# Transposes of probabilities and gate factors as two half blocks of 64 query rows, on halves of TensorE's array

## The chip, the cores and the metric

The kernel runs on one core of a Trainium2 chip. The time is the device time of one execution in microseconds (us), the median of repeated runs. Engines are named as the profile names them: PE is TensorE (PEld its weight loads), DVE is VectorE, ACT is ScalarE, POOL is GpSimd, SP is SyncE, which issues the DMAs.

## The reference, cut to what matters

Three layers follow one another on 2 sequences of 768 tokens, all in float32. First comes attention with 8 heads of 64 channels, over a window of 15 keys to either side and over the maxima or means of 24 blocks of 32 keys. Then comes a mixture of 4 experts, each a causal attention of its own with 64 channels, of which each token takes the best two, weighted by gates. Last is a feed-forward layer with token shift, 512 to 1024 to 512, squared ReLU and a sigmoid gate.

```python
a = np.exp(scores_all - max); a = a / (a.sum(-1) + 1e-9)      # layer 1: windowed and block keys together
x = np.matmul(a, v_all)
...
a = softmax(causal(scale * q @ k.T)); ye = a @ v @ wo[e]      # layer 2, expert e
out += mask * w * ye
...
k = np.maximum(xk @ w_k, 0.0); v = k * k @ w_v                # layer 3
return 1 / (1 + np.exp(-(xr @ w_r))) * v
```

## The kernel before, in words

**Turning the probabilities.** Softmax is computed with the query rows on the partitions. The product with the values wants the keys there. So each block of probabilities is turned by TensorE: a matmul with the block as weights and an identity as the moving operand, whose result lies in PSUM and has to be copied to SBUF before it can be used.

**Stage one** (`stage1`, L1331) works through 12 tiles of 128 queries. For each, `stage1_scores` (L556) makes the scores of 8 heads, 4 heads in each of two groups called `par`, with 120 keys each. `stage1_softmax` (L600) makes probabilities of them. `stage1_trans` (L633) turns the 4 blocks of one `par` into one PSUM bank (L652), which one copy of 512 columns takes out. `stage1_out` (L657) multiplies with the values (L670).

**The experts' attention** (`attention`, L819) works through 4 chunks of 384 queries, and in each through 2 pairs of experts (`ep`). `scores` (L827) makes the scores of both experts of a pair, which lie on the two halves of the partitions, with matmuls on half the rows of the array each (L845). `weights` (L870) makes the gate factors, one value for each query and expert, spread over 128 columns, and turns three blocks of them (L886). `attend` (L894) takes the blocks of probabilities in groups of three, two groups in the first chunk of a sequence and five in the second. `tr` (L899) turns one group of one expert into one bank (L905), and one copy of 384 columns takes it out. `vmm` (L920) multiplies a few groups with the values (L931), the two experts on the two halves of the array's columns.

**After that** come the output projection (L973), the gate of the last layer (`rec`, L1125), its first product (`hid`, L1176) and its second (`duo`, L1263), with splitting of operands into a high and a low part on VectorE, ScalarE and GpSimd (L371 to L381 and others). No block is turned there.

**Shapes of the array.** Each TensorE step notes a mode: full (128 x 128), half (two halves of the columns), rows (two halves of the rows) or quarter. Products with weights and all turns are full, the scores of the experts are rows, the products with values half, the scores of stage one quarter.

**The order of the work** is not that of the program. `Plan.op` (L240) only notes steps, numbered as they are noted, with their buffers, and `Plan.run` (L270) issues them in the order of the list `ORDER` (L53). An entry divided by four is the number of the step; the remainder chooses among the engines that the step allows. A step is issued as one piece. `HOMES` (L173) gives each buffer its slot. PSUM has 8 banks of 512 columns under the name `ps`. `rnd` (L370) is the helper of the copies, so they carry L371 (ScalarE), L372 (VectorE) or L374 (GpSimd). `several` (L400) gathers a few turns into one step.

Of the kernel before, what the change touches and what calls it, by code (L numbers as in the profile page):

```python
# [20 lines left out]
P = 128  # L21
# [29 lines left out]
GROUP = dict(p1=2, p1t=1, p1o=4)  # L51

ORDER = (  # L53
# [117 lines left out]
)  # L171

HOMES = (  # L173
# [1294 lines left out]
```

## Time and profile before

| what | value |
|---|---|
| median of 3 runs | 345.99 us (345.98 to 346.04) |
| the profiled execution | 346.08 us |
| its span, first to last instruction | 343.9 us |
| granted TensorE clock | 0.999 of full speed |
| busy share of PE, DVE, ACT, POOL | 95%, 93%, 77%, 29% |
| HBM traffic | 97 GB/s over the span |

The profile is of one execution. Busy time is the union of the records of an engine's instructions. A record runs from an instruction's start to its end, and the records of neighbours overlap, on TensorE above all. So what an instruction costs in a row of many is the distance from start to start.

### The profile page before, as it was taken

The numbers are of one execution on the slowest core, as the hardware profiler recorded it, in microseconds if no ns is written. First come the engines' busy times: TensorE is split into PE (matmuls) and PEld (weight loads), VectorE is DVE, ScalarE is ACT, GpSimd is POOL, SyncE is SP. The second block draws the span as 40 slices with busy tenths as digits, with TensorE's granted clock in tenths as the row PEclk, the third lists the DMA queues.
The fourth block names the chain that finished last, engine by engine and source line by source line (L and its number), as shares of the span: only waits on it lengthen the run. The fifth ranks groups of instructions, "written<-read, shape, count | busy, mean of one in ns | idle before, by whom it ended". The sixth has DMA issues, their size and how long they took to land.

```text
span 343.9 us, 8297 instructions
## 1 busy us (share of the span) xinstructions
PE 328.0 (95%) x3008; PEld 295.8 (86%) x3008; DVE 318.6 (93%) x927; ACT 264.5 (77%) x713; POOL 100.1 (29%) x124
## 2 busy tenths in 40 slices
PE   3799999999999999999999999999899999999995
PEld 2679988888789889888777999998799889999995
DVE  3799899999899899899999998999999999999995
ACT  0998889989979766668787698689697887876550
POOL 0554741774212533132120002600333001420450
PEclk9999999999999999999999999999999999999999
DMA  7994998655331001002131011000112000011113
GB/s 267 388 394 143 294 335 278 194 157 151 118 115 56 2 2 61 3 7 67 51 124 61 2 63 61 2 0 0 63 44 79 2 1 2 30 48 61 64 46 124
DMA packets 19624, 34.03 MB, mean 99 GB/s; under 512 B 2080, under 2 KB 8480, under 8 KB 19584
## 3 DMA queue, kind: packets, MB, share of 16 engines
q1 hardware_dynamic: 19584, 33.51, 29.0%
q8 instruction: 24, 0.39, 0.5%
q14 instruction: 16, 0.13, 0.1%
HBM read 30.16 MB, written 3.15 MB: 97 GB/s over the span
## 4 chain that ended last, share of the span: by engine, by line
PE 70%; DVE 21%; ACT 3%; issue 3%; DMA 2%; SPq 0%; DVEq 0%; ACTq 0%
PE ps L1263 15%; PE ps L745 9%; PE ps L905 5%; PE ps L763 5%; PE ps L931 5%; PE ps L973 5%; PE ps L1125 5%; PE ps L845 5%; PE ps L1176 4%; PE ps L670 3%; PE ps L652 3%; PE ps L586 2%; DVE b L379 2%; DVE b L1149 2%; DVE t L1102 2%
## 5 line engine op out<-in xcount | busy, mean ns | idle before, releaser
L1263 PE MATMUL ps<-w,s 128*128 128x256 f32 x336 | 49.2, 281 | 0.7 <-DVE s L379 0.6
L1263 PEld LDWEIGHTS ps<-w,s 128*128 128x128 f32 x336 | 44.0, 188 | 1.2 <-DVE s L379 1.1
L1176 PE MATMUL ps<-b,w 128*128 128x384 f32 x216 | 41.6, 340 | 2.3 <-ACT b L371 1.2
L1176 PEld LDWEIGHTS ps<-b,w 128*128 128x128 f32 x216 | 37.7, 188 | 4.3 <-ACT b L371 1.5
L745 PE MATMUL ps<-b,w 128*128 128x384 f32 x192 | 39.1, 345 | 0.0
L1125 PE MATMUL ps<-w,b 128*128 128x512 f32 x144 | 36.2, 399 | 0.0
L371 ACT ACTIVATE t<-ps 128x384 f32<-128x384 f32 (+1 forms) x62 | 26.9, 470 | 11.5 <-PE ps L905 6.5
L745 PEld LDWEIGHTS ps<-b,w 128*128 128x128 f32 x192 | 32.5, 189 | 0.3
L1125 PEld LDWEIGHTS ps<-w,b 128*128 128x128 f32 x144 | 26.4, 188 | 5.5 <-issue 0.2
L371 ACT ACTIVATE b<-ps 128x384 f32<-128x384 f32 (+4 forms) x53 | 25.4, 496 | 5.7 <-DVE t L1102 2.5
L612 ACT ACTIVATE w<-w,nm 128x120 f32<-128x120 f32 x72 | 27.7, 389 | 1.4 <-DVE nm L609 1.4
L371 ACT ACTIVATE b<-t 128x384 fp32r<-128x384 f32 x39 | 19.6, 522 | 5.1 <-DVE t L1102 2.5
L371 ACT ACTIVATE s<-u 128x512 fp32r<-128x512 f32 x24 | 14.9, 629 | 9.7 <-PE ps L1263 3.8
L1102 DVE SCALAR_TENSOR_TENSOR t<-b,mu,t 128x384 f32<-128x384 f32 x32 | 21.3, 684 | 1.2 <-ACT t L390 1.1
L763 PE MATMUL ps<-q,b 128*128 128x260 f32 x144 | 22.0, 293 | 0.0
L379 DVE TENSOR_TENSOR b<-t,b 128x384 fp32r<-128x384 f32 x39 | 21.9, 576 | 0.0
L381 POOL TENSOR_TENSOR w<-s,w 128x512 fp32r<-128x512 f32 x11 | 14.7, 1337 | 21.9 <-ACT w L371 10.7
L973 PE MATMUL ps<-u,w 128*128 128x384 f32 x96 | 21.0, 347 | 0.0
L381 POOL TENSOR_TENSOR b<-t,b 128x384 fp32r<-128x384 f32 x5 | 5.1, 1021 | 54.3 <-ACT b L371 54.2
L931 PE MATMUL ps<-t,b 128*64 128x384 f32 (+2 forms) x144 | 20.7, 422 | 0.0
L845 PE MATMUL ps<-ks,b 64*128 64x384 f32 (+3 forms) x192 | 19.3, 333 | 0.2 <-issue 0.2
L763 PEld LDWEIGHTS ps<-q,b 128*128 128x128 f32 x144 | 18.7, 188 | 0.8 <-issue 0.4
(203 smaller groups left out, 927.7 us busy)
## 6 DMA issues: line engine op xcount, KB each, us to landing
s<-in_wk SPq DMA_DIRECT2D x8, 512.0 KB, 4.1
s<-in_wv SPq DMA_DIRECT2D x8, 512.0 KB, 3.7
w<-in_vp SPq DMA_DIRECT2D x15, 256.0 KB, 6.1
w<-in_qT SPq DMA_DIRECT2D x12, 256.0 KB, 5.9
out_y<-t SPq DMA_DIRECT2D x24, 128.0 KB, 1.7
s<-in_wr SPq DMA_DIRECT2D x4, 512.0 KB, 6.1
s<-in_kS SPq DMA_DIRECT2D x6, 320.0 KB, 5.4
ks<-in_kS SPq DMA_DIRECT2D x4, 400.0 KB, 5.1
```

The source lines that it names most:

```text
L371: ways = [("act", act(n, sb), lambda: nc.scalar.activation(dst(), src(), AF.Copy)), ("dve", dve2(n) if sb else dve(n), lambda: nc.vector.t ...
L379: ways = [("dve", dve(n), lambda: nc.vector.tensor_tensor(dst(), a(), b().bitcast(F32), ALU.subtract), sb)]
L612: op("act", act(NK, True) + 186, lambda i=i, z=z, pr=pr, nm=nm: nc.scalar.activation(pr()[:, i], pr()[:, i], AF.Exp, bias=nm.t[:, i:i + 1] ...
L745: mm(p.t[:, :C], a[kc].t[:, cols], x.t[:, kc, :], start=(kc == 0 and i == 0), stop=(kc == KC - 1 and i == 2))
L763: mm(p.t[:, :260], x.t[:, kc, tok], a[kc].t, start=(kc == 0 and i == 0), stop=(kc == KC - 1 and i == 2))
L845: mm(ps[e2].t[:, :z - a], q1.t[r, x, tok], ks.t[r, y, a:z], start=n == 0, stop=n == 2)
L931: mm(acc.t[64 * e2:64 * e2 + 64, tq0 * P:(tq0 + cnt) * P], vv.t[:, kb, e * D:(e + 1) * D], th[e2].t[:, i0 * P:(i0 + cnt) * P], start=first ...
L973: mm(p.t[:, :C], a[ep].t[:, m * P:(m + 1) * P], x.t[:, ep, :], start=(ep == 0 and i == 0), stop=(ep == 1 and i == 2))
L1102: op("dve", dve(C) + 60, lambda: nc.vector.scalar_tensor_tensor(tmp(), cur(), mu.t[:, i:i + 1], tmp(), ALU.mult, ALU.add), r=rd, w=[(mb, m ...
L1125: mm(p.t, a.t[:, kc, tok], w[2](), start=(kc == 0 and i == 0), stop=(kc == KC - 1 and i == 2))
L1176: mm(p.t[:, :C], a[2]()[:, o:o + P], x.t[:, u, j], start=not (j or i), stop=j == 1 and i == 2)
L1263: mm(p.t[:, :256], x.t[:, u, j * P:(j + 1) * P], v[2]()[:, col:col + 256], start=not (j or i), stop=j == FC // 2 - 1 and i == 2)
```

## The change

Each turn of a 128-row block becomes two matmuls (`turn`): rows 0 to 63 of the block against the upper left 64 x 64 piece of the identity, and rows 64 to 127 against the lower right one. The two use different halves of the array's rows and write into two PSUM banks, 64 columns each. All turns get the mode rows.

In stage one the 8 blocks of a tile are turned into two banks, one for each half of the queries, in two steps of four blocks. The copies write every other stretch of 64 columns: four copies of 256 columns (for the first two tiles two of 512). The factors need two banks and two copies of 192 columns. In the experts' attention `tr` turns one group of both experts into two banks, in two steps of three blocks, with four copies of 192 columns.

`ORDER` and `HOMES` are rewritten as a whole. Counted in the two lists with the numbers of the steps:

| in the order | before | after |
|---|---|---|
| steps | 2156 | 2056 |
| TensorE steps | 642 | 458 |
| changes of mode from one TensorE step to the next | 61 | 88 |
| of these into rows | 14 | 36 |
| copies of turned blocks on ACT, on DVE | 70, 18 | 133, 39 |
| normalising steps of stage one on POOL (of 24) | 14 | 19 |
| splitting steps of `load_wk` and `load_wv` on POOL (of 96) | 20 | 29 |

```diff
-GROUP = dict(p1=2, p1t=1, p1o=4)
+GROUP = dict(p1=2, p1o=4)
+
+TURN = 62
...
-    def stage1_trans(t, par, state):
-        pk, pr = state[t, par]
-        pk = [(pk[0], (pk[1], i)) for i in range(4)] if t < EARLY else [pk] * 4
-        p = bank("ps")
...
-        for i in range(4):
-            several("p1t", GROUP["p1t"], i, 4, 109,
-                    lambda i=i: nc.tensor.transpose(p.t[:NK, i * P:(i + 1) * P], pr()[:, i], ident()),
-                    r=[pk[i], cst], w=[(p, i)], claim=(pt,))
-        rnd("act" if par else "dve", pa, lambda: p.t[:NK], 512, [p], [key])
-        state[t, par] = (key, pa)
+    def halfwise(v, n):
+        return v.rearrange("p (i q) -> p i q", i=n)
+
+    def turn(banks_, c, src):
+        for a in range(2):
+            r = slice(SUB * a, SUB * a + SUB)
+            v = src(r)
+            nc.tensor.transpose(banks_[a].t[:v.shape[1], c * SUB:(c + 1) * SUB], v, cst.t[r, r])
+
+    def stage1_trans(t, state):
+        p = [bank("ps"), bank("ps")]
+        pts = [buf("b6", [P, 2, 4 * P])] if t < 2 else [buf("w", [P, 4 * P]) for par in range(2)]
+        for par in range(2):
...
+            def go(par=par, pr=pr):
+                for i in range(4):
+                    turn(p, 4 * par + i, lambda r: pr()[r, i])
+
+            op("pe", TURN * 4, go, r=pk + [cst], w=[(x, par) for x in p], stream="p1t", claim=pts[-par:], mode="rows")
+        for a in range(2):
+            c = slice(SUB * a, SUB * a + SUB)
...
+            for par in range(2):
+                rnd("act" if a else "dve", lambda c=c, par=par: halfwise(pts[par].t[:NK], 4)[:, :, c],
+                    lambda a=a, par=par: halfwise(p[a].t[:NK, 256 * par:256 * par + 256], 4), 256, [p[a]],
+                    [(pts[par], a)])
...
-            p = bank("ps")
-            for tq in range(TPC):
-                several("p2f", TPC, tq, TPC, 109, lambda tq=tq: nc.tensor.transpose(
-                    p.t[:, tq * P:(tq + 1) * P], f.t[:, tq * P:(tq + 1) * P], ident()), r=[f, cst], w=[(p, tq)])
-            rnd("act", lambda: f.t, lambda: p.t[:, :C], C, [p], [f])
+            p = [bank("ps"), bank("ps")]
+
+            def go():
+                for tq in range(TPC):
+                    turn(p, tq, lambda r: f.t[r, tq * P:(tq + 1) * P])
+
+            op("pe", TURN * TPC, go, r=[f, cst], w=p, stream="p2f", mode="rows")
+            for a in range(2):
+                rnd("act", lambda a=a: halfwise(f.t, TPC)[:, :, SUB * a:SUB * a + SUB],
+                    lambda a=a: halfwise(p[a].t[:, :C // 2], TPC), C // 2, [p[a]], [(f, a)])
...
-            def tr(gi, e2):
-                p = bank("ps")
-                th = buf("t", [P, C])
-                for i, (kb, tq) in enumerate(groups[gi]):
-                    pr = prs[e2][tq]
-                    several("p2a", 1, i, len(groups[gi]), 109,
...
-                rnd("dve" if gi % 4 == 3 else "act", lambda: th.t, lambda: p.t[:, :C], C, [p], [th])
+            def tr(gi):
+                p = [bank("ps"), bank("ps")]
+                n = len(groups[gi])
+                th = [buf("t", [P, C]) for e2 in range(2)]
+                for e2 in range(2):
+                    def go(e2=e2):
+                        for i, (kb, tq) in enumerate(groups[gi]):
+                            turn(p, n * e2 + i, lambda r: prs[e2][tq].t[r, kb * P:(kb + 1) * P])
+
+                    op("pe", TURN * n, go, r=list(dict.fromkeys(prs[e2][tq] for kb, tq in groups[gi])) + [cst],
+                       w=[(x, e2) for x in p], stream="p2a", claim=th[:1 + e2], mode="rows")
+                for a in range(2):
+                    for e2 in range(2):
+                        rnd("dve" if gi % 4 == 3 else "act",
+                            lambda a=a, e2=e2: halfwise(th[e2].t[:, :n * P], n)[:, :, SUB * a:SUB * a + SUB],
+                            lambda a=a, e2=e2: halfwise(p[a].t[:, n * SUB * e2:n * SUB * (e2 + 1)], n), n * SUB,
+                            [p[a]], [(th[e2], a)])
                 return th
...
-                    ths[gi] = [tr(gi, e2) for e2 in range(2)]
+                    ths[gi] = tr(gi)
...
-                for par in range(2):
-                    stage1_trans(t, par, state)
+                stage1_trans(t, state)
```

## Rows read from the trace of the kernel before

**Rows 1.** The page's first part: busy us (share of the span) xinstructions.

```profile
PE 328.0 (95%) x3008; PEld 295.8 (86%) x3008; DVE 318.6 (93%) x927; ACT 264.5 (77%) x713; POOL 100.1 (29%) x124
```

**Rows 2.** Busy us by stretch: PE, PEld, DVE, ACT, POOL; then clock, DMA share, GB/s.

```profile
0.00:26.00 26.00, 17.65 (x430) 14.82 (x432) 17.52 (x91) 16.45 (x66) 9.24 (x21) 1.00 0.96 350
26.00:188.00 162.00, 161.32 (x1619) 139.08 (x1616) 151.82 (x543) 134.09 (x412) 57.33 (x80) 1.00 0.36 117
...
214.00:289.00 75.00, 71.97 (x402) 66.68 (x401) 74.10 (x137) 61.39 (x130) 17.24 (x15) 1.00 0.07 22
289.00:344.00 55.00, 51.07 (x430) 50.87 (x430) 50.45 (x109) 30.13 (x60) 15.01 (x8) 0.99 0.18 59
```

**Rows 3.** The chain of waits: shares of the span by engine; one piece (start, us, what).

```profile
PE 70%; DVE 21%; ACT 3%; issue 3%; DMA 2%; SPq 0%; DVEq 0%; ACTq 0%
...
53.98 4.23 PE ps L745 x24
```

**Rows 4.** The turns by line: count, duration min/median/max in ns, first and last start.

```profile
L652 PE MATMUL ps<-cst,w x72: 270/272/297, 38.2 to 115.4; 128*120 128x128 f32 x72
...
L905 PE MATMUL ps<-cst,u x72: 270/272/328, 52.6 to 181.0; 128*128 128x128 f32 x72
...
L886 PE MATMUL ps<-cst,t x24: 270/272/328, 66.4 to 187.4; 128*128 128x128 f32 x24
```

**Rows 5.** Timeline of PE, 38 to 47 us: start, length, line, tiles, form, count.

```profile
38.22 0.38 PE L652 MATMUL ps<-cst,w 128*120 128x128 f32 x2
38.36 1.81 PE L745 MATMUL ps<-b,w 128*128 128x384 f32 x9
...
41.82 1.80 PE L652 MATMUL ps<-cst,w 128*120 128x128 f32 x15
43.55 1.15 PE L670 MATMUL ps<-w,w 120*64 120x64 f32 x32
44.53 1.10 PE L670 MATMUL ps<-w,p 120*64 120x64 f32 x32
```

**Rows 6.** Groups by line and form: busy us, mean ns of one, idle before.

```profile
L745 PE MATMUL ps<-b,w 128*128 128x384 f32 x192 | 39.1, 345 | 0.0
...
L845 PE MATMUL ps<-ks,b 64*128 64x384 f32 x96 | 10.9, 346 | 0.0
...
L845 PE MATMUL ps<-ks,b 64*128 64x128 f32 x24 | 2.2, 272 | 0.2 <-issue 0.2
...
L745 PEld LDWEIGHTS ps<-b,w 128*128 128x128 f32 x192 | 32.5, 189 | 0.3
...
L845 PEld LDWEIGHTS ps<-ks,b 64*128 64x128 f32 x192 | 14.9, 185 | 2.5 <-issue 0.8 <-ACT b L371 0.2 <-ACT s L1014 0.2
...
L905 PEld LDWEIGHTS ps<-cst,u 128*128 128x128 f32 x72 | 9.5, 141 | 0.8 <-issue 0.5
...
L670 PE MATMUL ps<-w,w 120*64 120x64 f32 x224 | 7.5, 223 | 0.0
...
L670 PEld LDWEIGHTS ps<-w,w 120*64 120x64 f32 x224 | 7.0, 138 | 0.5 <-DVE t L372 0.2 <-issue 0.2
```

**Rows 7.** Timeline of PE around 76.9 and 116.8 us, entries into the half-row shape.

```profile
76.74 0.27 PE L905 MATMUL ps<-cst,u 128*128 128x128 f32 x1
76.94 1.32 PE L845 MATMUL ps<-ks,b 64*128 64x384 f32 x12
...
116.77 0.55 PE L845 MATMUL ps<-ks,b 64*128 64x128 f32 x6
```

**Rows 8.** Copies on ACT: two groups by form, then the timeline at 140 us.

```profile
L371 ACT ACTIVATE t<-ps 128x384 f32<-128x384 f32 x50 | 22.5, 493 | 8.6 <-PE ps L905 6.5 <-PE ps L886 1.8
...
L371 ACT ACTIVATE t<-ps 128x256 f32<-128x256 f32 x12 | 4.4, 373 | 2.9 <-PE ps L1263 2.9
...
140.13 0.50 ACT L371 ACTIVATE b<-ps 128x384 f32<-128x384 f32 x1
140.50 0.51 ACT L371 ACTIVATE ks<-ps 128x384 fp32r<-128x384 f32 x1
```

More of the change, by code (lines that the diff above doesn't have):

```diff
@@ L631, in stage1_softmax @@
                             ("act", 4 * 290, norm_act)], r=[(rss, k)], w=key)
-    def stage1_trans(t, par, state):
-        pk, pr = state[t, par]
-        pk = [(pk[0], (pk[1], i)) for i in range(4)] if t < EARLY else [pk] * 4
-        p = bank("ps")
-        if t < 2:
-            if par == 0:
-                state["early"] = buf("b6", [P, 2, 4 * P])
-            pt = state["early"]
-            key = (pt, par)
-            def pa():
-                return pt.t[:NK, par]
-        else:
-            pt = key = buf("w", [P, 4 * P])
-            def pa():
-                return pt.t[:NK]
-        for i in range(4):
-            several("p1t", GROUP["p1t"], i, 4, 109,
-                    lambda i=i: nc.tensor.transpose(p.t[:NK, i * P:(i + 1) * P], pr()[:, i], ident()),
-                    r=[pk[i], cst], w=[(p, i)], claim=(pt,))
-        rnd("act" if par else "dve", pa, lambda: p.t[:NK], 512, [p], [key])
-        state[t, par] = (key, pa)
+    def halfwise(v, n):
+        return v.rearrange("p (i q) -> p i q", i=n)
@@ new lines, in turn @@
+    def turn(banks_, c, src):
[7 more added lines that the diff above has]
+        for par in range(2):
+            pk, pr = state[t, par]
+            pk = [(pk[0], (pk[1], i)) for i in range(4)] if t < EARLY else [pk]
+            def go(par=par, pr=pr):
[4 more added lines that the diff above has]
+            c = slice(SUB * a, SUB * a + SUB)
+            if t < 2:
+                rnd("act" if a else "dve",
+                    lambda a=a, c=c: halfwise(pts[0].t[:NK].rearrange("p a n -> p (a n)"), 8)[:, :, c],
+                    lambda a=a: halfwise(p[a].t[:NK], 8), 512, [p[a]], [(pts[0], a)])
+                continue
+            for par in range(2):
+                rnd("act" if a else "dve", lambda c=c, par=par: halfwise(pts[par].t[:NK], 4)[:, :, c],
+                    lambda a=a, par=par: halfwise(p[a].t[:NK, 256 * par:256 * par + 256], 4), 256, [p[a]],
+                    [(pts[par], a)])
+        for par in range(2):
+            state[t, par] = ((pts[0], lambda par=par: pts[0].t[:NK, par]) if t < 2 else
+                             (pts[par], lambda par=par: pts[par].t[:NK]))
@@ L897, in attend @@
             acc = bank("ps")
-            def tr(gi, e2):
-                p = bank("ps")
-                th = buf("t", [P, C])
-                for i, (kb, tq) in enumerate(groups[gi]):
-                    pr = prs[e2][tq]
-                    several("p2a", 1, i, len(groups[gi]), 109,
-                            lambda i=i, kb=kb, pr=pr: nc.tensor.transpose(
-                                p.t[:, i * P:(i + 1) * P], pr.t[:, kb * P:(kb + 1) * P], ident()),
-                            r=[pr, cst], w=[(p, i)], claim=(th,))
-                rnd("dve" if gi % 4 == 3 else "act", lambda: th.t, lambda: p.t[:, :C], C, [p], [th])
+            def tr(gi):
[14 more added lines that the diff above has]
+                            [p[a]], [(th[e2], a)])
                 return th
```

283 rows, old and new, of tables (HOMES, ORDER) are left out of this document.

## The prediction

> **What bounds the kernel now.** I read the totals first. TensorE is busy for 95% of the span and VectorE for 93% [rows 1]. Such averages mix stages, so a table by stretch comes next [rows 2]. Between 26 and 188 us, where all but the first of the turns lie, TensorE works for 161.32 of 162 us: little else can be the limit there. VectorE is idle for 162 - 151.82 = 10.2 us of that stretch, ScalarE for 27.9, GpSimd for 104.7. From 214 to 289 us it is VectorE that is full (74.10 of 75), and after 289 TensorE again until the last additions. The chain of waits says the same in one line: 70% of the span lies on TensorE, 21% on VectorE [rows 3]. So a us taken from TensorE before 188 us can count, as long as VectorE, with 10.2 us to spare, follows.
>
> **The turns themselves.** There are 96 in stage one (12 tiles of 8), 168 of the experts' probabilities (28 pairs of groups, 6 each) and 24 of gate factors: 288; one row of each line stands here [rows 4]. Each has a matmul record of about 272 ns, but records overlap, so the price is the distance between starts. Fifteen in a row last 1.80 us, the last record 0.27 of it: (1.80 - 0.27) / 14 = 109 ns each [rows 5]. Put between products of the same full shape they cost no more: two turns start at 38.22 and the next products at 38.36, 0.14 later; that run of nine lasts 1.81 where eight distances of 4.23 / 24 = 0.176 and a record of 0.345 make 1.75, so two turns took 0.20 [rows 3, 5, 6].
>
> After the change a turn is two matmuls, each with 64 rows of the array, 128 (or 120) columns of weights and 64 moving columns. No row shows exactly that. Two neighbours bound it. Above: L845 has the same half-row shape, both halves in step; its six matmuls with 128 columns take 0.55 us with a record of 0.27, so two distances of pairs in 0.28 [rows 6, 7]; less some 0.05 for the entry into the shape (below) that is 115 ns a pair, no cheaper than one full turn. Below: L670 moves 64 f32 columns in two column halves; 32 matmuls, 16 pairs, last 1.10 us with records of 0.223, so (1.10 - 0.22) / 15 = 58.5 ns a pair [rows 5, 6]. I take 59, because what limits L845 there is its weight load: a 128-column load has a record of 185 ns at L845 and 189 at L745, one of 64 columns 138 at L670, and the 128-column load of a turn 141 [rows 6]. A turn's load is thus as short as a 64-column one, it hides behind 64 moving columns, and the moving columns, which halve, set the pace. Gain: 288 x (109 - 59) = 14.4 us. Bounds: 14.5 (58.5), and a loss of 288 x (115 - 109) = 1.7 us.
>
> The rule against this stands in the Trainium skill, "TensorE: Matmul & The Clock Gate", section "LDWEIGHTS (loading the stationary operand)": a load takes time by its columns, P / 1.2 ns, however few rows it has. For 128 columns that is 107 ns, and the turns would then gain next to nothing; that the records of 185 and 138 ns part by 47 ns fits it (53 by the rule), the 141 ns record of a turn does not.
>
> **The shape changes.** A turn used to have the shape of the products around it. Now it has the half-row shape of the scores, and going in and out of a shape costs. After fifteen turns the next start is due at 41.82 + 15 x 0.109 = 43.46; L670, another shape, starts at 43.55, 0.09 late, and its first 16 pairs take 0.98 us where 16 x 0.0585 = 0.94 were due: 0.13 to 0.14 us for one change [rows 5]. Into L845 at 76.94 it is 0.09 late too, and then six pairs take (1.32 - 0.35) / 5 = 0.194 each where a 384-column product takes 0.176, 5 x 0.018 = 0.09 more: 0.18 [rows 3, 6, 7]. I take 0.15, nearer the first, since a turn's load is short. The new order, counted step by step in the diff, has 88 changes of shape against 61; those into the half-row shape go from 14 to 36. So 27 x 0.15 = 4.1 us back (bounds 3.6 and 4.9). Net on TensorE: 14.4 - 4.1 = 10.3 us less.
>
> **The copies out of PSUM.** They move the same elements in more instructions: 88 copies become 172, since a half bank holds half of each query block. ScalarE's 384-wide copies have records of 0.493 us, the 256-wide ones 0.373: 0.94 ns an element, and 0.13 us that does not shrink with the width. Back to back they start 0.37 apart (140.13, 140.50), of which the elements account for 384 x 0.00094 = 0.36, so nearly all of the fixed part can overlap: 0.01 is left [rows 8]. So 84 more copies cost 0.8 to 10.9 us. By the new order 133 of the 172 go to ScalarE and 39 to VectorE (70 and 18 before): 63 x 0.01 to 0.13, 0.6 to 8.2 us, beside 27.9 us that ScalarE idles, and 21 more, 0.2 to 2.7 us, into VectorE's 10.2. I cost them at nothing on the path: TensorE's other work covers them. If that cover is gone, it is rival two.
>
> **What is queued behind what.** Both heads of a pair now share two banks, so a copy waits for the turns of both, and the product with the values waits for four copies rather than two. On TensorE that product is queued behind the turns in the order; while it waits, the steps behind it wait too. The factors claim two banks for one. No DMA is moved, and none waits for a turn. The order is rewritten as a whole: GpSimd gets more of the normalising (19 of 24 for 14) and of the weight splitting (29 of 96 for 20), for which it has 104.7 us of idle time, and VectorE is spared some.
>
> **Sum.** After 188 us nothing of the change runs, so 214 to 289 keeps its length and only starts earlier. Of the 10.3 us I hand back the share that the chain spends on VectorE, a fifth, 2.1 us: closing VectorE's gaps without a loss would need all of its 10.2 us. That leaves 8.2. The profiled execution took 346.08 us (span 343.9 and 2.2 around it), 0.09 above the median of 345.99: 346.08 - 8.2 = **337.9 us**.
>
> **Rivals.**
> - *VectorE becomes the bound.* It has 10.2 us of gaps where TensorE gives up 10.3, and takes 21 more copies. For: 93% busy, and full between 214 and 289. Against: in that later stretch it runs at 74.10 of 75, so such filling is possible. With half of the gaps closed, 5.1 us are gained: 341.0 us.
> - *The copies come late and TensorE waits for them.* For: ScalarE already waits for turns, and each product with values now needs four copies. Against: 27.9 us of idle ScalarE. With the 84 extra copies all on the path at the full 0.13, 10.3 - 10.9 leaves it 0.6 us slower, 346.7; at half of that price 10.3 - 5.5 = 4.8 us are gained, 341.3; in the middle 344.0 us.
> - *The halves do not run faster than one full turn* (other sign). The place is the weight load: if the half loads of 128 columns take as long as L845's, a pair costs 109 ns or more and the 27 changes of shape are pure loss: 346.08 + 4.1 = 350.2, and at 115 ns a pair 1.7 more, 351.9; 351 us in the middle. It decides from a pair distance of 95 ns upward, where 288 x 14 ns are the 4.1 us. For: the 115 ns at L845. Against: 141 ns beside 185. This would also be the change not doing what it says.
>
>   The rule of the Trainium skill named above ("TensorE: Matmul & The Clock Gate", LDWEIGHTS) would bring this about.
> - *More than the sum.* The new order may also fill some of TensorE's 8.35 us of idle time before 26 us. With no hand-back and the cheap change of shape, 346.08 - 14.5 + 3.6 = 335.2; with a fifth of those 8.35 as well, 333.5.
>
> **How the numbers follow.** Forecast, 335.2 to 340: 0.55. Below 335.2: 0.08. VectorE, 340 to 342: 0.17. Copies late, 342 to 346.7: 0.11, of which 0.04 falls within 0.2% (0.7 us, about what a measurement of this kernel can tell from no change) and 0.01 beyond it. Half loads, near 351: 0.09. So faster 0.86, same 0.04, slower 0.10. For 8 in 10 the range runs from 333.5 to 344.0; it leaves out the half loads and the worst of the copies.
>
> **What would show each step.** In the changed profile, halves of a pair should start a few ns apart and pairs about 59 apart, with weight-load records near 140 ns; pairs 109 apart would sink the forecast. TensorE's busy time should fall from 328.0 to about 318, and 26 to 188 us should end near 180, with VectorE above 95% there. Copies of 192 columns should show records of about 0.31 us. The stretch filled by VectorE and the last one of TensorE should keep their 75 and 55 us. If TensorE shows gaps that end with a copy, the second rival holds; if VectorE has none left and TensorE has some, the first.

## The result and the profile after

The changed kernel takes **332.98 us** (median of 4 runs, 332.38 to 333.85), against 345.99 (345.70 to 346.04): a ratio of 0.963 (95% interval 0.9605 to 0.965). The forecast was 337.9 and the range ended at 333.5, so the gain of 13.0 us is 1.6 times the 8.2 foretold. The profiled execution took 332.78 us with a span of 331.0; its span is 12.9 us shorter than before.

First the page of the changed kernel: busy us, share and instructions of each engine, and the chain of waits by engine.

```profile
PE 319.1 (96%) x3296; PEld 286.8 (87%) x3296; DVE 311.3 (94%) x941; ACT 266.8 (81%) x777; POOL 114.0 (34%) x127
...
PE 94%; DVE 2%; DMA 2%; SPq 1%; issue 0%; ACT 0%; ACTq 0%
```

TensorE is busy for 8.9 us less than in [rows 1], where the forecast had 10.3. The chain is the surprise. It lay on VectorE for 21% of the span [rows 3]; now that is 2%. GpSimd works 13.9 us more, VectorE 7.3 less.

To see where the time went, the span is cut where the same work begins in both kernels: at 26 us, at the first matmul of the hidden layer (`hid`, L1176 before and L1197 after), and at the first of its second product (`duo`, L1263 and L1284). The table by stretch, columns as in [rows 2], of the kernel before:

```profile
26.00:192.60 166.60, 165.92 (x1641) 143.10 (x1638) 156.42 (x552) 137.56 (x419) 57.33 (x80) 1.00 0.35 114
192.60:279.00 86.40, 84.07 (x442) 78.10 (x441) 84.39 (x163) 71.72 (x153) 16.89 (x15) 1.00 0.09 31
279.00:344.00 65.00, 60.37 (x505) 59.74 (x503) 60.25 (x124) 38.81 (x78) 16.69 (x9) 0.99 0.15 50
```

and of the changed kernel:

```profile
0.00:26.00 26.00, 18.02 (x450) 15.08 (x452) 17.00 (x95) 15.70 (x62) 10.39 (x22) 1.00 0.95 344
26.00:184.90 158.90, 158.73 (x1904) 133.32 (x1901) 152.78 (x559) 140.42 (x489) 66.06 (x82) 1.00 0.37 121
184.90:266.70 81.80, 81.80 (x442) 78.28 (x441) 80.78 (x164) 72.80 (x153) 22.13 (x16) 1.00 0.10 33
266.70:331.00 64.30, 60.51 (x508) 60.13 (x507) 60.75 (x126) 37.86 (x76) 15.45 (x8) 1.00 0.15 50
```

Up to the hidden layer 192.6 us became 184.9, 7.7 less. The hidden layer's stretch, in which no block is turned and TensorE has the same 442 matmuls, became 4.6 us shorter, 81.8 for 86.4. The last stretch lost 0.6. So a third of the gain came where the prediction allowed for none. That stretch was VectorE's before, idle for only 2.01 us of it; now TensorE is busy for all of its 81.80.

The turns themselves, by line (the turns' helper; records in ns, minimum, median, maximum):

```profile
L637 PEld LDWEIGHTS ps<-cst,u x144: 136/139/143, 55.0 to 174.8; 64*128 64x128 f32 x144
L637 PE MATMUL ps<-cst,u x144: 221/222/225, 55.1 to 174.9; 64*128 64x64 f32 x144
```

and in the timeline of TensorE (start, length, line, tiles, form, count):

```profile
37.77 0.68 PE L637 MATMUL ps<-cst,w 64*120 64x64 f32 x16
38.38 3.43 PE L754 MATMUL ps<-b,w 128*128 128x384 f32 x18
41.74 0.68 PE L637 MATMUL ps<-cst,w 64*120 64x64 f32 x16
42.35 1.15 PE L679 MATMUL ps<-w,p 120*64 120x64 f32 x32
```

The weight load's record is 139 ns, close to the 141 that [rows 6] had for a full turn. Sixteen halves, eight pairs, last 0.68 us, of which a record is 0.22: (0.68 - 0.22) / 7 = 66 ns a pair, the slow first pair included. Inside a run the two halves of a pair mostly start 3 ns apart. Behind the first pair, which takes about 109 ns, pairs start 59 ns apart in stage one (120 columns of weights) and 62 elsewhere (128).

### The profile page after: what moved, and what is told of

It is laid out like the page before. It is cut to its first block, busy times and chain, and to the rows that moved or that the text cites. A ratio compares the mean times of both kernels' runs of the same rounds, so it can differ in the third digit from the quotient of the medians.

```text
span 331.0 us, 8978 instructions
## 1 busy us (share of the span) xinstructions
PE 319.1 (96%) x3296; PEld 286.8 (87%) x3296; DVE 311.3 (94%) x941; ACT 266.8 (81%) x777; POOL 114.0 (34%) x127
## 4 chain that ended last, share of the span: by engine, by line
PE 94%; DVE 2%; DMA 2%; SPq 1%; issue 0%; ACT 0%; ACTq 0%
PE ps L1284 18%; PE ps L1197 18%; PE ps L754 11%; PE ps L1146 10%; PE ps L637 6%; PE ps L952 6%; PE ps L772 6%; PE ps L854 6%; PE ps L994 5%; PE ps L679 3%; PE ps L583 3%; DMA ks<-in_kS 2%; PE ps L588 1%; PE ps L500 1%; DVE w L606 1%; SPq L359 1%
## 5 line engine op out<-in xcount | busy, mean ns | idle before, releaser
L1284 PE MATMUL ps<-w,s 128*128 128x256 f32 x336 | 48.7, 281 | 0.0
L1284 PEld LDWEIGHTS ps<-w,s 128*128 128x128 f32 x336 | 43.9, 188 | 0.1
L1197 PE MATMUL ps<-b,w 128*128 128x384 f32 x216 | 40.3, 337 | 0.0
L1197 PEld LDWEIGHTS ps<-b,w 128*128 128x128 f32 x216 | 38.0, 188 | 0.1
L368 ACT ACTIVATE t<-ps 128x192 f32<-128x192 f32 (+1 forms) x108 | 30.9, 356 | 8.6 <-PE ps L637 4.2
L754 PE MATMUL ps<-b,w 128*128 128x384 f32 x192 | 36.6, 341 | 0.0
L754 PEld LDWEIGHTS ps<-b,w 128*128 128x128 f32 x192 | 33.2, 188 | 0.9 <-issue 0.4
L368 ACT ACTIVATE b<-ps 128x384 f32<-128x384 f32 (+4 forms) x50 | 23.8, 492 | 3.9 <-PE ps L994 1.6
L854 PE MATMUL ps<-ks,b 64*128 64x384 f32 (+3 forms) x192 | 21.8, 342 | 0.0
L368 ACT ACTIVATE w<-ps 120x256 f32<-120x256 f32 (+2 forms) x49 | 19.7, 445 | 1.7 <-PE ps L1146 0.8
L376 DVE TENSOR_TENSOR b<-t,b 128x384 fp32r<-128x384 f32 x37 | 20.1, 567 | 0.5 <-ACT b L368 0.3
L772 PE MATMUL ps<-q,b 128*128 128x260 f32 x144 | 20.3, 290 | 0.2 <-DVE b L376 0.2
L994 PE MATMUL ps<-u,w 128*128 128x384 f32 x96 | 18.9, 338 | 0.0
L387 ACT ACTIVATE t<-b,omu 128x384 f32<-128x384 f32 x28 | 16.9, 613 | 2.2 <-PE ps L952 1.6
```

The source lines that it names most:

```text
L368: ways = [("act", act(n, sb), lambda: nc.scalar.activation(dst(), src(), AF.Copy)), ("dve", dve2(n) if sb else dve(n), lambda: nc.vector.t ...
L376: ways = [("dve", dve(n), lambda: nc.vector.tensor_tensor(dst(), a(), b().bitcast(F32), ALU.subtract), sb)]
L754: mm(p.t[:, :C], a[kc].t[:, cols], x.t[:, kc, :], start=(kc == 0 and i == 0), stop=(kc == KC - 1 and i == 2))
L772: mm(p.t[:, :260], x.t[:, kc, tok], a[kc].t, start=(kc == 0 and i == 0), stop=(kc == KC - 1 and i == 2))
L854: mm(ps[e2].t[:, :z - a], q1.t[r, x, tok], ks.t[r, y, a:z], start=n == 0, stop=n == 2)
L994: mm(p.t[:, :C], a[ep].t[:, m * P:(m + 1) * P], x.t[:, ep, :], start=(ep == 0 and i == 0), stop=(ep == 1 and i == 2))
```

## The experiments

Each kernel ran beside the kernel before on the same chip; ratios are to that one. That neighbour took 345.99 us beside the changed kernel, but 346.78 beside four of the experiments (the turns done twice, the 104 turns left out in the new order, and the two that exchange engines). Where one of these four is compared with the changed kernel, the difference of the times is given first, and then the difference of the two gains over the neighbours.

In the sums below, TensorE's work up to the hidden layer is its busy time in the first two stretches: 17.65 + 165.92 = 183.57 us before, 18.02 + 158.73 = 176.75 after. Such a sum is good to about 3 us: where the two experiments below exchange only the engines of steps, with the same matmuls in the same order, it is 18.03 + 167.80 = 185.83 for 183.57 and 17.15 + 162.76 = 179.91 for 176.75.

### What a turn and a change of shape cost

**The changed kernel with the experts' turns done twice.** It prices a pair without a further change of shape, and shows whether TensorE's time counts in full in the new order.

```diff
                         for i, (kb, tq) in enumerate(groups[gi]):
-                            turn(p, n * e2 + i, lambda r: prs[e2][tq].t[r, kb * P:(kb + 1) * P])
+                            for again in range(2):
+                                turn(p, n * e2 + i, lambda r: prs[e2][tq].t[r, kb * P:(kb + 1) * P])
```

> The changed kernel, with each of the 168 turns of the experts' probabilities done twice in place: 168 x 0.062 = 10.4 us more on TensorE, about what the change took from it, everything else as it is. If in the new order TensorE is the bound throughout, 333.0 + 10.4 = 343.4 (342 to 345): then the new order alone is worth some 3 us and the faster turns the rest. If the new order brought nothing of its own, 346 or more. If VectorE or ScalarE carries part of the bound, below 341.5.

Measured: 343.53 us (342.12 to 345.02), ratio 0.990 (0.987 to 0.993). In its trace the distances from the start of a turn's half to the next matmul add up to 31.55 us, in the changed kernel to 21.18: 10.4 us for 168 pairs, **62 ns a pair**. The time rose by 343.53 - 332.98 = 10.6 us, or by 13.01 - 3.25 = 9.8 by the gains: all of it, or nearly all. Its hidden-layer stretch is again 81.8 us. With TensorE busy for 328.6 us in all, as in the kernel before (328.0), it is still 3.2 us faster than its neighbour before: that much the new order gives without any saving on TensorE.

**The kernel before with each turn cut to its first half.** Old order, one half-row matmul for each turn: many changes of shape, each half alone.

```diff
...
-                                p.t[:, i * P:(i + 1) * P], pr.t[:, kb * P:(kb + 1) * P], ident()),
+                                p.t[:, i * P:i * P + SUB], pr.t[:SUB, kb * P:(kb + 1) * P], cst.t[:SUB, :SUB]),
...
```

> The kernel before in its old order, each turn cut to its first half (64 rows of the array, 64 moving columns), which takes the time of a pair of halves; the copies keep number and width and read the half block twice, so half of the probabilities and factors is left out. Turns: 288 x (109 - 59) = 14.4 us less on TensorE. But the old order has 146 changes of shape with half-row turns, against 61. At 0.15 us a change 85 x 0.15 = 12.8 us more: 346.0 - 1.6 = 344.4. At 0.10 a change 340; at 0.19 347.8. Theory A (shape changes cost about what the prediction took, and the new order is needed to gather the turns): 342.5 to 346. A rival by which a change of shape is hidden behind other work: below 339.

Measured: 351.29 us (349.90 to 351.37), ratio 1.0145 (1.0116 to 1.0174): slower than either theory had it. The timeline of TensorE has the half turns alone, and a run of 15 of them:

```profile
40.03 0.33 PE L652 MATMUL ps<-cst,w 64*120 64x64 f32 x2
40.29 0.80 PE L750 MATMUL ps<-b,w 128*128 128x384 f32 x3
...
42.19 1.10 PE L652 MATMUL ps<-cst,w 64*120 64x64 f32 x15
```

(1.10 - 0.22) / 14 = 63 ns, the slow first one included: one half takes as long as a pair, so all that a pair gains is that its halves run side by side. Between products of the full shape, the next product starts 0.26 us after two half turns start (40.03 to 40.29), where it started 0.14 after two full turns (38.22 to 38.36 in [rows 5]): halving them made them dearer there. TensorE's work up to the hidden layer rose by 3.6 us, to 187.15. The trace of before gives its 288 turns 29.64 us from start to start, 103 ns each; 288 x (103 - 63) = 11.5 us should have gone, and the trace has 145 changes of shape for 60. So 85 changes cost 15.1 us, **0.18 us** each, or 0.14 to 0.21 with the 3 us by which such a sum can be off. The Trainium skill, "TensorEngine Tiling (Array Packing)", section "Key Properties", says that going from one tiling mode to another drains TensorE; it gives no price. The price in this case is the one just worked out.

**The changed kernel with all blocks of a step turned on one half first, then on the other.**

```diff
-    def turn(banks_, c, src):
-        for a in range(2):
-            r = slice(SUB * a, SUB * a + SUB)
...
+    def turn(banks_, blocks):
+        for n in range(2):
+            a = side[0] ^ n
+            for c, src in blocks:
+                r = slice(SUB * a, SUB * a + SUB)
...
+        side[0] ^= 1
```

> The changed kernel with its own order, copies, banks and shape changes; only within a step all blocks are turned for one half of the rows and then all for the other, so the two halves meet once per step and no longer pair by pair. A step of four blocks then takes 7 distances of about 59 ns in place of 4 of 62, one of three blocks 5 in place of 3: 24 x 0.165 + 64 x 0.109 = 10.9 us more on TensorE. Theory A (the halves side by side are what TensorE gained, the new order closed its gaps on VectorE's stretch by itself): TensorE stays the bound, 333.0 + 10.9 = 343.9, between 342.5 and 345. Theory B (the new order brought nothing of its own, all came with TensorE's time): with TensorE's work back to within 0.5 us of the kernel before, the gaps come back too, 346 or more. If VectorE bounds the changed kernel already, less than 341.

Measured: 333.77 us (332.94 to 335.58), ratio 0.9655 (0.9618 to 0.9693), level with the changed kernel. The 10.9 us more that the expectation put on TensorE did not come (its work up to the hidden layer is 18.60 + 159.08 = 177.68 us for 176.75), so its theories were not put to the test. Four blocks of one half now stand ahead of four of the other in the program, yet the run in the timeline hardly grew:

```profile
40.95 0.75 PE L641 MATMUL ps<-cst,w 64*120 64x64 f32 x16
41.63 0.57 PE L683 MATMUL ps<-w,p 120*64 120x64 f32 x12
```

In that run most starts still come in twos, 2 to 16 ns apart, with 43 to 60 ns to the next, but for 94 behind the first two. Matmuls on one half alone started 63 ns apart in the mean (the experiment above). So two within 16 ns should be on different halves, the first two of the run as well, which the program has on the same half: it looks as if the halves ran as two streams of their own, and a matmul started ahead of ones that stand before it in the program on the other half. The records don't tell on which half a matmul was, so this is inferred. How the program interleaves the pairs is not where the gain comes from. The Trainium skill ("TensorE: Matmul & The Clock Gate", Part 3, "What overlaps and what doesn't") has matmuls start strictly in program order; read in this way, these starts don't fit that.

**The changed kernel with 104 of its 288 turns left out**, to see what a still cheaper turn would bring.

```diff
-                for i in range(4):
+                for i in range(0, 4, 2):
...
-                            turn(p, n * e2 + i, lambda r: prs[e2][tq].t[r, kb * P:(kb + 1) * P])
+                            i == 1 or turn(p, n * e2 + i, lambda r: prs[e2][tq].t[r, kb * P:(kb + 1) * P])
```

> The changed kernel with the same 104 of 288 turns left out as in the run of the old order with fewer turns (copies keep number and width and read other blocks again): 104 x 0.062 = 6.4 us less on TensorE. If TensorE still bounds the changed kernel: 333.0 - 6.4 = 326.6. If VectorE is level with it by now, as it was in the old order, where 11.3 us less on TensorE gave 3.8: a third, 331.

Measured: 332.37 us (331.59 to 332.97), ratio 0.9588 (0.9555 to 0.962). 104 x 62 ns = 6.4 us of turns should be gone; the trace has 5.5 us less of them (15.7 for 21.18 from start to start). The time fell by 0.6 us, or by 14.41 - 13.01 = 1.4 by the gains: far less than the 6.4, and less than the third that the expectation gave as its other case. The chain of this run lies less on TensorE:

```profile
PE 76%; DVE 9%; ACT 6%; DMA 5%; issue 2%; SPq 1%; DVEq 0%; ACTq 0%
```

The change has thus taken most of what the turns had to give: with less work, TensorE waits for the others.

### Whether the extra copies cost anything

**The changed kernel with one full-width copy in place of two half-width ones** (88 copies for 172; the 92 and 80 of the expectation should be 88 and 84). `one` copies the first bank to both halves for `a` of 0, and issues nothing for 1.

```diff
...
-                rnd("act" if a else "dve", lambda c=c, par=par: halfwise(pts[par].t[:NK], 4)[:, :, c],
-                    lambda a=a, par=par: halfwise(p[a].t[:NK, 256 * par:256 * par + 256], 4), 256, [p[a]],
-                    [(pts[par], a)])
+                one(a, "act" if a else "dve", lambda par=par: pts[par].t[:NK],
+                    lambda par=par: p[0].t[:NK, 256 * par:256 * par + 256], 4, [p[a]], [(pts[par], a)])
...
```

> The changed kernel, where one copy of full width reads the first bank twice over and its partner is left out, so that 92 copies move the elements of 172 (in the first two tiles nothing is changed); half of each turned block is not used. If the extra copies are covered by other work (the prediction's step): within 0.7 us of 333.0. If they lie on the path: 80 of them at 0.01 to 0.13 us, 0.8 to 10.4 us faster, in the middle 327.5.

Measured: 334.66 us (333.30 to 335.74), ratio 0.9684 (0.965 to 0.9718): nothing gained. The 84 extra copies lie under other work, as the forecast said. The median is 1.7 us longer, but the granted clock of its runs differs: one run took 333.30 us at 1.00 of full speed, the other three 334.08 to 335.74 at 0.995 to 0.997, while all of the changed kernel's runs were at 0.999 or 1.00. So no loss is shown either. The changed kernel's 192-column copies are, by form (busy us, mean ns, idle before):

```profile
L368 ACT ACTIVATE t<-ps 128x192 f32<-128x192 f32 x96 | 26.8, 353 | 4.5 <-PE ps L637 4.2
```

Their mean of 0.353 us is above the 0.31 that the prediction gave as the sign to look for.

### Whether the old order would have kept the gain

**The kernel before, old order, with 104 of its 288 turns left out.**

```diff
-                    lambda i=i: nc.tensor.transpose(p.t[:NK, i * P:(i + 1) * P], pr()[:, i], ident()),
+                    lambda i=i: i % 2 or nc.tensor.transpose(p.t[:NK, i * P:(i + 1) * P], pr()[:, i], ident()),
...
-                            lambda i=i, kb=kb, pr=pr: nc.tensor.transpose(
+                            lambda i=i, kb=kb, pr=pr: i == 1 or nc.tensor.transpose(
```

> The kernel before in its old order, with 104 of its 288 turns left out (the second and fourth of each four in stage one, the middle one of each three of the experts); the copies keep their number and width and read other blocks again, so the output is not the reference's. TensorE loses 104 x 0.109 = 11.3 us of work, with no change of shape added. Theory A: the old order's VectorE stretch keeps its TensorE gaps of 3 us and VectorE hands back something before it: 335 to 338. Theory B: time taken from TensorE shows in full and the gaps close as well: 346.0 - 11.3 - 2.9 = 331.8, at most 334.

Measured: 342.21 us (341.20 to 344.85), ratio 0.990 (0.987 to 0.993). 104 x 103 ns = 10.7 us less for TensorE, about the net gain that the forecast had from the turns (the trace has 20.3 us of turns for 29.64, so 9.4 less), brought 3.8 us, less than either theory. About three fifths were handed back: up to the hidden layer (now at 188.7) TensorE idles for 12.7 us, before for 9.0; the hidden-layer stretch keeps its length at 86.7, and the chain leaves TensorE:

```profile
PE 45%; DVE 30%; ACT 13%; DMA 7%; issue 3%; SPq 1%; ACTq 0%; DVEq 0%
```

**The new order with the old choice of engines.** An entry of `ORDER` divided by four is the step and the remainder picks its engine. 42 steps of the changed kernel were set back to the engine that they had before: 14 fewer for GpSimd, 15 more for VectorE. The order of the steps stays.

```diff
-    552, 468, 448, 540, 528, 452, 84, 344, 696, 348, 568, 456, 476, 576, 148, 352, 712, 356, 544, 680, 460, 560,
+    552, 468, 448, 540, 528, 452, 84, 344, 696, 348, 568, 457, 476, 576, 148, 352, 712, 356, 544, 680, 460, 560,
```

> The changed kernel in its order, with the engines of 42 steps (normalising in stage one, and the splitting of the last layer's weights) set back as in the kernel before: 14 steps fewer on GpSimd, 15 more on VectorE. Theory A1 (the new order's relief for VectorE is the work it gave to GpSimd): 15 steps of 0.35 to 0.6 us, 2 to 5 us slower, 335 to 338. Theory A2 (it is where the steps stand, and which VectorE steps GpSimd slows): within 1 us, 332 to 334.

Measured: 342.41 us (341.86 to 342.52), ratio 0.9875 (0.9846 to 0.9905), **9.4 us slower than the changed kernel** (8.6 by the gains), though every turn is new: about twice what theory A1 had at most, and far from theory A2. The table by stretch shows where:

```profile
26.00:194.50 168.50, 162.76 (x1924) 134.97 (x1924) 161.09 (x575) 141.94 (x491) 58.16 (x71) 1.00 0.35 115
194.50:276.30 81.80, 81.80 (x442) 78.29 (x441) 80.70 (x164) 73.22 (x154) 22.12 (x16) 1.00 0.10 33
```

VectorE has 161.09 us of work up to the hidden layer for 152.78, and TensorE waits 5.7 us there where it waited 0.2. All of the loss lies in this stretch; the hidden layer keeps its 81.8.

**The old order with the new choice of engines**, the same 42 steps the other way round.

> The kernel before in its order with full turns, with the same 42 steps given to the engines that the new order gives them (14 more on GpSimd). Theory A1: VectorE's stretch before the last product is relieved, 342 to 344.5. Theory A2: within 0.7 us of 346.0, or slower, since the steps stand where VectorE has to wait for GpSimd.

Measured: 348.73 us (348.07 to 349.81), ratio 1.006 (1.004 to 1.009): 2 us slower than before, as theory A2 allows. So the engines' choice is worth 9 us inside the order that was made for it and less than nothing outside. Here too the hidden-layer stretch stays as the old order has it, 86.5 us.

### What shortened the hidden layer's stretch

In all ten kernels so far (the two compared and eight experiments) its length went with the order of the steps alone: 86.4 to 86.7 us in the four with the old order, 81.8 in the six with the new one. Something in the order had to be found. The timeline of the kernel before, VectorE from 242 to 249 us:

```profile
241.47 1.02 DVE L1194 TENSOR_TENSOR b<-ps,b 128x384 f32<-128x384 f32 x2
242.40 1.53 DVE L1022 SCALAR_TENSOR_TENSOR s<-s,s 128x512 int32<-128x512 int32 x1
...
245.72 3.18 DVE L1102 SCALAR_TENSOR_TENSOR t<-b,mu,t 128x384 f32<-128x384 f32 x3
```

and GpSimd beside it:

```profile
242.36 1.03 POOL L381 TENSOR_TENSOR b<-t,b 128x384 fp32r<-128x384 f32 x1 [20.33 <-ACT b L371]
246.10 1.38 POOL L1039 TENSOR_TENSOR u<-ks 128x512 f32<-128x512 f32 x1 [2.71 <-ACT ks L1187]
247.43 1.06 POOL L381 TENSOR_TENSOR q<-s,q 128x256 fp32r<-128x256 f32 x1
```

The three instructions of L1102 take 3.18 us here, 0.61 each where GpSimd is idle (their median). The last ends at 248.90, 0.41 after GpSimd's last at 248.49. Added up over the records, VectorE instructions that lie beside GpSimd ones took 6.8 us more than the median of their form in this stretch before, 3.2 after (7.9 with the one that starts at 287 us, behind the stretch). The Trainium skill, "SBUF — State Buffer", section "Who interferes with whom", says that a VectorE instruction with two SBUF inputs and a GpSimd one that reads SBUF shut each other out for the whole instruction. The records nearly agree: the lengthened ones end 0.41 to 0.55 us after a GpSimd record ends (243.94 after 243.39, 247.90 after 247.48, 248.90 after 248.49), a little less than the 0.61 to 0.68 that they take alone. Two kernels try whether it is what held the stretch.

**The kernel before, GpSimd's two-tensor instructions cut to 32 columns.**

```diff
-                     ("pool", pool_tt(n), lambda: nc.gpsimd.tensor_tensor(dst(), a(), b(), fn))], r=r, w=w)
+                     ("pool", pool_tt(n), lambda: nc.gpsimd.tensor_tensor(few(dst()), few(a()), few(b()), fn))], r=r, w=w)
+
+    def few(v):
+        return v[:, :32] if len(v.shape) == 2 else v
```

> The kernel before, in its old order and with its old turns; GpSimd's tensor-tensor adds and subtracts in the elements that either engine may take work on 32 columns alone (the rest of those elements' columns is left out), so that little of GpSimd runs beside VectorE there. Theory A (what lengthened the stretch from the first hidden-layer matmul to the first matmul of the last stage in the old order is VectorE instructions that take about 0.5 us longer beside GpSimd's tensor-tensor ones, 7.9 us of such lengthening there before against 3.2 after): most of that goes, the stretch falls from 86.4 to between 82 and 83.5 us, and the time is 340 to 343.5. Theory B (the stretch is longer because of where the order puts its steps on the two engines, whatever each instruction takes): the stretch stays within 1 us of 86.4, and the time is 345 or more.

Measured: 342.71 us (342.35 to 343.20), ratio 0.9903 (0.9878 to 0.9929). The time is theory A's, the stretch is neither's:

```profile
192.20:276.70 84.50, 83.24 (x443) 78.27 (x442) 81.11 (x165) 71.98 (x153) 8.99 (x15) 1.00 0.10 32
```

It takes 84.5 us, 1.9 of the 4.6 less. But 2.4 us of lengthening were left, since the instructions at 240 to 246 us are others and were not cut; the chain of waits still leaves TensorE from 233 to 247 us, right there. So the next kernel takes them as well.

**The kernel before, GpSimd copying one tensor in place of adding or subtracting two.**

```diff
+    def one(dst, a):
+        return nc.gpsimd.tensor_scalar(dst, a, 1.0, 0.0, ALU.mult, ALU.add)
...
-            ways.append(("pool", pool_tt(n), lambda: nc.gpsimd.tensor_tensor(
-                dst(), a(), b().bitcast(F32), ALU.subtract)))
+            ways.append(("pool", pool_tt(n), lambda: one(dst(), a())))
...
-                     ("pool", pool_tt(n), lambda: nc.gpsimd.tensor_tensor(dst(), a(), b(), fn))], r=r, w=w)
+                     ("pool", pool_tt(n), lambda: one(dst(), a()))], r=r, w=w)
```

> The kernel before, old order and old turns, with every add and subtract of two tensors on GpSimd that either engine may take replaced by a copy of the first one with the same columns (the second operand is left out, so the low parts and sums made there aren't what they should be). GpSimd still writes as much, but reads one tensor. Theory A (VectorE loses its time beside GpSimd instructions that read two tensors, and that is what holds the stretch from the first hidden-layer matmul to the last stage): nearly all of the lengthening goes, in the stretch 6.8 us of it, and the stretch falls below the 84.5 of the run with 32 columns, to 82 to 83.5 us; time 338 to 342. Theory B (the rest of the difference, 84.5 against 81.8 us, is where the old order puts its steps): the stretch stays between 84 and 85, the piece of the chain on ScalarE and VectorE from 233 to 247 us stays, and the time is 342 to 343.5.

Measured: 340.20 us (339.87 to 341.37), ratio 0.9836 (0.9816 to 0.9856). The stretch, the same place on VectorE, and GpSimd beside it:

```profile
192.20:274.90 82.70, 82.70 (x443) 78.35 (x442) 79.66 (x165) 72.00 (x153) 9.55 (x15) 1.00 0.11 33
```

```profile
240.10 0.87 DVE L1024 SCALAR_TENSOR_TENSOR s<-s,s 128x512 int32<-128x512 int32 x1
240.89 0.75 DVE L382 TENSOR_TENSOR b<-t,b 128x384 fp32r<-128x384 f32 x1
...
242.96 1.66 DVE L1104 SCALAR_TENSOR_TENSOR t<-b,mu,t 128x384 f32<-128x384 f32 x3
...
246.74 0.54 DVE L1196 TENSOR_TENSOR b<-ps,b 128x384 f32<-128x384 f32 x1
```

```profile
239.81 0.62 POOL L379 TENSOR_SCALAR u<-ks 128x512 f32<-128x512 f32 x1
240.39 0.84 POOL L379 TENSOR_SCALAR q<-s 128x256 fp32r<-128x256 f32 x1
246.51 0.68 POOL L379 TENSOR_SCALAR b<-b 128x384 f32<-128x384 f32 x1 [5.27 <-DVE b L1196]
```

The three instructions of the line that was L1102 take 1.66 us for 3.18; GpSimd is done before they start. The stretch is 82.7 us long, **3.7 of the 4.6 us**, with old turns, old order and old engines; TensorE is busy for all of it, and the chain lies on TensorE for 95% of the span. So VectorE's lost time beside GpSimd is what held this stretch. GpSimd's own steps became shorter too (9.55 us there for 16.89), but that is no rival: in the kernel before, no piece of the chain from 192 to 280 us lies on GpSimd. Theory A's wording was a little off: a GpSimd instruction that reads one tensor lengthens VectorE's two-input ones too (0.87 for 0.68, 0.75 for 0.55 us at 240), but most are about half as long as before. The instruction at 246.74 has one input in PSUM and keeps its 0.54 us beside GpSimd.

**The changed kernel with the same edit.**

> The changed kernel with the same edit: GpSimd's adds and subtracts of two tensors become copies of the first (the second operand is left out). In the changed kernel 10.0 us of VectorE's time lie in instructions lengthened beside GpSimd, 3.2 of them between the first hidden-layer matmul and the last stage. Theory A (TensorE alone sets the end there): the stretch stays at 81.8 us and the time within 0.7 us of the changed kernel's. Theory B (VectorE, level with TensorE, holds some of the end): the time falls by 1 us or more, before the first hidden-layer matmul.

Measured: 333.39 us (332.78 to 334.43), ratio 0.9643 (0.9625 to 0.9662), the changed kernel's time, as theory A has it, and a stretch of 81.8 us. VectorE's busy time fell by 3.5 us, to 307.8, and nothing came of it. The new order has already put GpSimd's work where VectorE can bear it. In the changed kernel's stretch it is GpSimd's records that are long, up to 3.18 us where others of the same form take 1.02, while VectorE keeps its pace beside them:

```profile
244.71 1.02 POOL L1060 TENSOR_TENSOR b<-b,b 128x384 f32<-128x384 f32 x1 [13.48 <-PE ps L1197]
249.21 3.18 POOL L1060 TENSOR_TENSOR b<-b,b 128x384 f32<-128x384 f32 x1
249.21 0.56 DVE L1059 TENSOR_TENSOR b<-b,b 128x384 f32<-128x384 f32 x1
```

As less work for TensorE alone brought 0.6 to 1.4 us above, neither of the two would be worth much shortened alone now; no run pointed to a version faster than the changed one.

## Why the prediction was wrong on the size

**The turns: right.** A pair was put at 59 ns by its short weight load; it takes 59 to 62, with a load record of 139 ns for the 141 of [rows 6], and halves 3 ns apart. The rival of half loads at 109 ns or more is out.

**The gain of 14.4 us: too large.** 109 ns was read in a run of fifteen [rows 5]; over the whole trace a turn took 103 from start to start, since some stood where the next start came sooner, as the two at 38.22 did. 288 x (103 - 62) = 11.8 us.

**The changes of shape, 4.1 us back: right in kind, perhaps too small.** TensorE's work up to the hidden layer fell by 183.57 - 176.75 = 6.8 us, so 11.8 - 6.8 = 5.0 us came back. Put on the 27 changes alone that is 0.19 each, near the 0.18 of the half turns and of the dearer of the prediction's two rows [rows 7]. But it is a remainder of sums that can be off by some 3 us, so 0.15 is not ruled out, and how the missing 3.5 us divide between the turns and the changes is an estimate. Net on TensorE: 6.8 us where 10.3 stood.

**The copies at nothing: right.** Fewer of them gained nothing. The rival in which TensorE waits for copies is out: from 26 us to the hidden layer it idles for 158.90 - 158.73 = 0.2 us in all. The rival in which VectorE becomes the bound is out by the same row: VectorE has 158.90 - 152.78 = 6.1 us of gaps left there.

**"Of the 10.3 us I hand back the share that the chain spends on VectorE, a fifth, 2.1 us": wrong.** In the old order the share handed back was about three fifths when turns were left out. In the new one it is nothing: TensorE's idle time up to the hidden layer fell from 9.03 to 8.15 us, and doubled turns cost all or nearly all of their price. What was only mentioned in the prediction, that GpSimd gets more and VectorE is spared some, is what made room inside the new order: with the engines set back in it, 8.6 to 9.4 us are lost. The two errors, 3.5 too much on TensorE and 2.1 + 0.9 too little here, nearly cancel by luck: 7.7 us up to the hidden layer, where 8.2 were foretold.

**"After 188 us nothing of the change runs, so 214 to 289 keeps its length and only starts earlier": this is the step that failed.** No turn runs there, but a part of the change does: the rewritten order. The hidden layer's stretch (192.6 to 279 us, most of that 214 to 289) lost 4.6 us, nearly the whole distance of 4.9 between forecast and result. The rows showed half of the sign, VectorE full beside a GpSimd at work [rows 2]; the other half stands in the timeline of that stretch, where instructions take 1.53 and 1.65 us in place of 0.68 and 0.61. The prediction read the stretch as filled by VectorE's work, and did not ask how much of that work was lost beside GpSimd. TensorE is busy for all of the stretch in the copying kernel as in the changed one; the remaining 0.9 us of the 4.6 were not traced to one cause.

The fourth rival, "more than the sum", had the right side for the wrong reason: it looked for the rest ahead of 26 us, where 0.4 us of TensorE's idle time went.

## What to carry to other kernels

When a change brings a rewritten order, that order is a term of the sum by itself, in the stretches that the named edit never touches too. Where an engine looks full, compare each of its instructions with the median of its form before calling the time work: what exceeds it may be given back by an order alone. And price an instruction that is removed by its mean over the whole trace, not by its run of many; what an engine's time is worth has a direction as well (here 104 turns less gave 0.6 to 1.4 of about 6 us, turns done twice took 9.8 to 10.6 for 10.4).

## What the runs showed of the hardware

The two row halves of the array seem to take their matmuls as two streams: with 4 of one half ahead of 4 of the other in the program, most starts still came in twos, 2 to 16 ns apart, where one half alone starts every 63 ns. One 64-row half alone takes as long for its turn (63 ns in a run of 15) as both together (66 in a run of eight pairs). A VectorE instruction with two inputs in SBUF took up to 1.0 us longer beside one on GpSimd (1.65 for 0.61 us at 246 us of the kernel before), and one on GpSimd up to 2.2 us longer beside VectorE (3.18 for 1.02 us at 249 us of the changed kernel).
